# A gated linear recurrence with a dense block behind it: prefix products over the whole sequence in place of pairwise joins of blocks

## The chip, the core and the metric

The kernel runs on one core of a Trainium2 chip. A core has five engines that run side by side, each through its own instructions in order: TensorE (PE in the profile; PEld is its loading of weights), VectorE (DVE), ScalarE (ACT), GpSimd (POOL) and SyncE (SP), which here only starts transfers. The metric is the device time of one execution in microseconds (us), lower is better; the figure is the median of three executions.

## The reference

Inputs `q, k, v, a_re, a_im` are float32 of shape (4, 8, 768, 48): batch B, heads H, steps S, width D. The two weight matrices are float64.

```python
mag = np.sqrt(a_re * a_re + a_im * a_im)
scale = np.minimum(mag, 0.999) / (mag + 1e-06)
a_re_n, a_im_n = (a_re * scale, a_im * scale)
for t in range(S):                                   # complex state S_re + i S_im, D x D per head
    new_re = ar * S_re - ai * S_im                   # ar, ai: a_re_n, a_im_n at step t, per row
    new_im = ar * S_im + ai * S_re
    kv = np.einsum('bhd,bhe->bhde', k[:, :, t], v[:, :, t])
    S_re, S_im = (new_re + kv, new_im)
    y[:, :, t] = np.einsum('bhd,bhde->bhe', q[:, :, t], S_re)
x = y as 3072 tokens of 384
h = x @ w_in                                         # 384 -> 2048
r = np.maximum(h, 0.0)
return (r * r) @ w_out                               # 2048 -> 384
```

In the inputs, `a_re` is uniform between 0.85 and 0.95 and `a_im` is normal with deviation 0.1, so a step shrinks the state by about a tenth.

## The kernel before

Work goes in **units** of one batch, two heads and 384 steps (32 units), and two units make a duo. A unit has head and dim on the 128 partitions (two heads of 48, each padded to 64) and steps along the free axis. It is cut into 3 chunks of 128 steps.

The score of step t with an earlier step s is Re(q_t k_s times the decay from s to t). No decay is ever divided by: blocks of w = 1, 2, 4, .. 64 steps are joined in pairs, seven levels, and each level multiplies `Q` (on DVE), `K` (on POOL) and the blocks' whole decays `T` (on DVE) by complex factors. `times` does one such product in four instructions, lines L297 (two), L300 and L302; `join` calls it:

```python
def join(u, w):
    ...
    times(dve, new, T[:, :, :, 0], ..., (n,), False, "t")
    times(dve, Q, Q, decay(0), (n, w), False, "q")
    ...
        times(pool, K, K, decay(1), (n, w), True, "k")
```

Ahead of each join, `small_scores` (L256 on PE, 32 x 32 pieces, gathered by a masked copy on DVE, L259) or `wide_scores` (L274) take that level's scores. Then `states` (L343 to L367) carries a state between chunks, `outputs` (L380, L385) forms y, and, per 384 tokens, the dense part runs on PE: `turn_x` (L395), `hidden` (L402, 16 blocks of 3 matmuls of 128 x 384) with relu and square on ACT (L405, L406), and `project` (L412, 3 blocks of 16). `normalise` (L205 to L224) prepares `a`, `load` (L180 to L192) starts the transfers on SP, and the weights come in 32 pieces by POOL's queue (L134) and are rounded from float64 by seven DVE instructions a piece (L139 to L151).

The order is written out: units two by two, level by level, with one piece of `work` (weights, then the dense part of the group before) after each level by `some`. A tile framework then fixes each engine's order of instructions, and puts in the waits.

Of the kernel before, what the change touches and what calls it, by code (L numbers as in the profile page):

```python
# [9 lines left out]
F32 = mybir.dt.float32  # L10
I32 = mybir.dt.int32
U32 = mybir.dt.uint32
AF = mybir.ActivationFunctionType
ALU = mybir.AluOpType
PSUM = bass.MemoryType.PSUM


@with_exitstack
def kernel(
# [11 lines left out]
    """y_t = q_t . Re(S_t), S_t = a_t S_{t-1} + k_t v_t, then relu(y w_in)^2 w_out.  # L31

    Within a chunk of 128 steps, the decay from s to t is a product that never leaves
    what it multiplies: blocks of w steps are joined in pairs, w = 1, 2, .. 64.  Before
    a join, Q holds q_t times the decay from the start of t's block up to t, K holds the
    conjugate of k_s times the decay from s to the end of s's block, and T holds each
    block's whole decay; so Re(Q K) is the score of each t of a right block with each s
    of the left block beside it.  Nothing is divided by a decay, and no logarithm is
    taken, so any a will do.  The state S (kept conjugated) passes between chunks.

    The weights may come in float64, as the raw 8 bytes: they are rounded to float32, the
    widest type that the engines compute in, on the chip.

    A unit is one batch, two heads and 384 steps: head, dim on the partitions (a head
    from 0, the other from 64, each with 16 rows of zeros), steps along the free axis.
    """
    nc = tc.nc
    B, H, S, D = q.shape
    C = 128
    NC = 3  # L50
    L = NC * C
    NHALF = S // L
# [3 lines left out]
    DM = H * D  # L56
    FF = moe_w_in.shape[1]
    NM = DM // C
# [27 lines left out]
    # masks[w][s mod 32, t]: 1 where s is in a left block of w steps and t in the right  # L86
    # block beside it (w = 0: s = t), for each of the four blocks of 32 partitions.
# [21 lines left out]
    # keeps a head's rows of the state to that head's columns  # L109
# [6 lines left out]
    # score tiles [s, (head, chunk), t]; the places with s > t stay zero  # L116
# [12 lines left out]
    def load_f64(dst, src):  # L129
        """dst = src, each the two words of a float64, rounded to float32; dst is 0 where  # L130
        that would not be a normal number"""
        shape = list(dst.shape)
        raw = wst.tile(shape + [2], U32, name="raw", tag="raw")
        nc.gpsimd.dma_start(out=raw.rearrange("p a b two -> p a (b two)"), in_=src)  # L134
        lo, hi = raw[:, :, :, 0], raw[:, :, :, 1]
        bits = dst.bitcast(U32)
        more = wst.tile(shape, U32, name="more", tag="more")
        # sign, exponent and the upper 20 bits of the fraction
        dve.tensor_scalar(out=bits, in0=hi, scalar1=0x07FFFFFF, scalar2=3,  # L139
                          op0=ALU.bitwise_and, op1=ALU.logical_shift_left)  # L140
        dve.scalar_tensor_tensor(out=bits, in0=hi, scalar=0xC0000000, in1=bits,
                                 op0=ALU.bitwise_and, op1=ALU.bitwise_or)
        # the lower 32, in units of the exponent
        dve.tensor_scalar(out=more, in0=bits, scalar1=0xFF800000, scalar2=None,
                          op0=ALU.bitwise_and)
        dve.scalar_tensor_tensor(out=more.bitcast(F32), in0=lo, scalar=2.0 ** -52,
                                 in1=more.bitcast(F32), op0=ALU.mult, op1=ALU.mult)
        dve.tensor_tensor(out=dst, in0=dst, in1=more.bitcast(F32), op=ALU.add)
        dve.tensor_scalar(out=more, in0=hi, scalar1=1, scalar2=None,
                          op0=ALU.logical_shift_left)  # L150
        dve.scalar_tensor_tensor(out=dst, in0=more, scalar=float(2 * 897 << 20), in1=dst,  # L151
                                 op0=ALU.is_ge, op1=ALU.mult)
# [42 lines left out]
    def normalise(u):  # L195
        """a *= min(|a|, 0.999) / (|a| + 1e-6)"""
# [11 lines left out]
        # the root's table wants its input in its range; then one Newton step  # L208
# [17 lines left out]
    def turn(u):  # L226
        """steps from the partitions to the free axis"""
# [14 lines left out]
    def small_scores(u, w):  # L242
        """scores of blocks of w within blocks of 32, gathered in u["A"]"""
# [19 lines left out]
    def wide_scores(u, w):  # L263
        """scores of blocks of 32 or 64, straight to their place"""
# [21 lines left out]
    def times(eng, dst, x, t, shape, conj, tag):  # L286
        """dst = x * t or x * conj(t), complex; dst may be x"""
# [17 lines left out]
    def join(u, w):  # L305
        """blocks of w to blocks of 2 w"""
# [26 lines left out]
    def states(u):  # L333
        """S before each chunk of the unit, and the one after it"""
# [137 lines left out]

# [28 lines left out]
```

## Time and profile before

| | |
|---|---|
| times of three runs | 1626.14 us median (1620.57 to 1630.79) |
| profiled execution, first to last instruction | span 1629.0 us |
| DVE busy | 1292.8 us, 79% of the span |
| PE busy | 1124.1 us, 69%, granted clock 0.824 in the mean |
| POOL busy | 848.4 us, 52% |
| ACT busy | 380.6 us, 23% |
| packets moved | 44.02 MB, 27 GB/s in the mean |

The profiled execution is one of its own, not one of the three; its span lies inside their range, 2.9 us above the median. "Busy" counts instructions that run, not those that wait. In a row of the timeline the first two numbers are start and duration; two instructions of one engine overlap a little, so the cost of one in a row of them is the distance from its start to the next one's. In a group's row, "x448 | 293.2, 661 | 0.0" means 448 instructions, 293.2 us busy, 661 ns for one in the mean, and no idle time of the engine ahead of them.

### The profile page before, as it was taken

What the parts mean: (1) busy time and instruction counts of PE and PEld (TensorE: products, weight loads), DVE (VectorE), ACT (ScalarE), POOL (GpSimd) and SP (SyncE); (2) the same over time, 40 slices, a digit from 0 to 9 for tenths busy, and PEclk for the clock granted to TensorE, in tenths of its full rate; (3) what the DMA queues carried; (4) which work ended last, traced back from release to release, by engine and by line L of the source; (5) the groups of instructions that cost most, each with busy time, mean ns of one, the idle gap of its engine ahead of it and who ended that gap; (6) DMA issues with size and microseconds to landing.
All of it is one profiled execution on the core that took longest, in us unless ns stands there. A gap on an engine that the chain in (4) does not pass through costs nothing.

```text
span 1629.0 us, 48569 instructions
## 1 busy us (share of the span) xinstructions
PE 1124.1 (69%) x20840; PEld 765.1 (47%) x20840; DVE 1292.8 (79%) x2922; ACT 380.6 (23%) x858; POOL 848.4 (52%) x1119
## 2 busy tenths in 40 slices
PE   2116215767877769767877779766877779676999
PEld 2115114545454546444454546444554546454565
DVE  6999998998959795988859794988859794979600
ACT  3012010232123311322123311222213321222131
POOL 5653764666627372555637372656537371656400
PEclk9997555878787979778888979778888969778899
DMA  4113212102020100102020200102020200100000
GB/s 93 54 36 82 64 40 64 34 2 39 7 48 2 34 6 21 34 2 39 6 48 3 38 3 23 31 2 39 6 48 3 39 2 26 29 1 3 11 5 14
DMA packets 137301, 44.02 MB, mean 27 GB/s; under 512 B 131456, under 2 KB 134528, under 8 KB 137088
## 3 DMA queue, kind: packets, MB, share of 16 engines
q1 hardware_dynamic: 134016, 28.34, 9.0%
q0 software_dynamic: 3072, 12.58, 2.5%
q8 instruction: 164, 2.69, 0.6%
q14 instruction: 49, 0.40, 0.1%
HBM read 36.18 MB, written 4.72 MB: 25 GB/s over the span
## 4 chain that ended last, share of the span: by engine, by line
DVE 58%; PE 23%; POOL 6%; issue 6%; ACT 4%; DMA 1%; SPq 1%; DVEq 0%; POOLq 0%; ACTq 0%
DVE q L297 13%; PE o L412 11%; DVE t L297 9%; DVE Q L300 6%; DVE Q L302 6%; DVE s L220 4%; PE h L402 3%; DVE A L259 3%; DVE T L300 3%; PE kv L348 2%; DVE T L302 2%; PE y L380 2%; DVE s L215 2%; PE y L385 2%; POOL k L297 2%
## 5 line engine op out<-in xcount | busy, mean ns | idle before, releaser
L297 POOL TENSOR_TENSOR k<-K,T 128x384 f32<-128x384 f32 x384 | 429.6, 1134 | 145.4 <-DVE T L302 57.8
L256 PE MATMUL lv<-Q,K 64*32 64x32 f32 x13824 | 178.8, 222 | 282.8 <-DVE Q L300 134.3
L402 PE MATMUL h<-xT,w 128*128 128x384 f32 x768 | 351.3, 607 | 2.3 <-DVE xT L396 2.3
L256 PEld LDWEIGHTS lv<-Q,K 64*32 64x32 f32 x13824 | 156.2, 121 | 361.5 <-POOL k L297 150.5
L297 DVE TENSOR_TENSOR q<-Q,T 128x384 f32<-128x384 f32 x448 | 293.2, 661 | 0.0
L412 PE MATMUL o<-w,g 128*128 128x384 f32 x768 | 281.9, 524 | 0.0
L402 PEld LDWEIGHTS h<-xT,w 128*128 128x128 f32 x768 | 168.7, 234 | 105.6 <-issue 46.3
L412 PEld LDWEIGHTS o<-w,g 128*128 128x128 f32 x768 | 152.9, 205 | 102.0 <-issue 18.3
L297 DVE TENSOR_TENSOR t<-T 128x384 f32<-128x384 f32 (+6 forms) x448 | 190.9, 459 | 0.0
L274 PE MATMUL lv<-Q,K 64*32 64x32 f32 (+1 forms) x2304 | 72.3, 236 | 162.4 <-DVE Q L300 136.0
L300 POOL TENSOR_TENSOR K<-k,k 128x192 f32<-128x192 f32 x192 | 136.8, 713 | 69.3 <-PE lv L274 64.9
L274 PEld LDWEIGHTS lv<-Q,K 64*32 64x32 f32 (+1 forms) x2304 | 59.6, 144 | 198.7 <-issue 128.3
L239 DVE TENSOR_TENSOR Q<-T,q 128x768 f32<-128x768 f32 x32 | 30.6, 956 | 150.5 <-ACT T L237 150.5
L300 DVE TENSOR_TENSOR Q<-q,q 128x192 f32<-128x192 f32 x224 | 138.5, 618 | 3.3 <-PE lv L274 3.0
L302 POOL TENSOR_TENSOR K<-k,k 128x192 f32<-128x192 f32 x192 | 135.6, 706 | 0.7 <-PE lv L256 0.7
L302 DVE TENSOR_TENSOR Q<-q,q 128x192 f32<-128x192 f32 x224 | 129.7, 579 | 0.0
L405 ACT ACTIVATE g<-h 128x384 f32<-128x384 f32 x128 | 62.3, 486 | 284.0 <-PE h L402 283.9
L185 POOL MEMSET kn<- 128x96 f32 x32 | 5.8, 182 | 196.2 <-PE tp L236 195.0
L284 ACT COPY score<-A 32x192 f32<-32x192 f32 x128 | 44.7, 349 | 151.3 <-DVE A L259 150.2
L207 POOL TENSOR_TENSOR s<-s,s 128x288 f32<-128x288 f32 x32 | 32.7, 1021 | 75.3 <-ACT s L206 75.3
L351 DVE TENSOR_TENSOR add<-kv,own 128x288 f32<-128x288 f32 (+1 forms) x64 | 25.7, 401 | 56.6 <-PE kv L348 56.2
L211 ACT ACTIVATE s<-s 128x288 f32<-128x288 f32 x32 | 14.1, 440 | 235.7 <-DVE s L209 235.7
(86 smaller groups left out, 1637.1 us busy)
## 6 DMA issues: line engine op xcount, KB each, us to landing
raw<-in_moe_w_in_dram POOLq DMA_DIRECT2D x16, 384.0 KB, 3.9
raw<-in_moe_w_out_dram POOLq DMA_DIRECT2D x16, 384.0 KB, 3.3
a<-in_a_re_dram SPq DMA_DIRECT2D x96, 48.0 KB, 2.2
a<-in_a_im_dram SPq DMA_DIRECT2D x96, 48.0 KB, 2.8
qn<-in_q_dram SPq DMA_DIRECT2D x96, 48.0 KB, 2.3
kn<-in_k_dram SPq DMA_DIRECT2D x96, 48.0 KB, 2.2
v<-in_v_dram SPq DMA_DIRECT2D x96, 48.0 KB, 2.0
out_dram<-o SPq DMA_DIRECT2D x24, 192.0 KB, 1.9
```

What stands on the lines that cost most here:

```text
L207: pool.tensor_tensor(out=s1, in0=s1, in1=s2, op=ALU.add)
L220: dve.reciprocal(out=s3, in_=s3)
L256: nc.tensor.matmul(ps[ts(i, SB), h, ts(c, SB)], lhsT=u["K"][rows, j, cols], rhs=rhs, start=(j == 0), stop=(j == parts[-1]))
L259: dve.copy_predicated(out=u["A"].rearrange("p (h c) t -> p h (c t)", h=2), mask=masks[w].rearrange("p (h c) t -> p h c t", h=2), data=ps[: ...
L274: nc.tensor.matmul(ps[lo:lo + w, h, ts(c, w)], lhsT=u["K"][rows, j, left], rhs=u["Q"][rows, j, right], start=(j == 0), stop=(j == 1))
L284: act.copy(out=u["score"][ts(i, SB), :, ts(i, SB)], in_=u["A"][ts(i, SB)])
L297: eng.tensor_tensor(out=f, in0=x, in1=part, op=ALU.mult)
L300: eng.tensor_tensor(out=dst[:, 0], in0=ra[:, 0], in1=rb[:, 1], op=ALU.add if conj else ALU.subtract)
L302: eng.tensor_tensor(out=dst[:, 1], in0=ra[:, 1], in1=rb[:, 0], op=ALU.subtract if conj else ALU.add)
L402: nc.tensor.matmul(ps, lhsT=w1[:, m, ts(f, C)], rhs=g["xT"][:, m], start=(m == 0), stop=(m == NM - 1))
L405: act.activation(out=t, in_=ps, func=AF.Relu)
L412: nc.tensor.matmul(ps, lhsT=g["h"][f][:, ts(c, C)], rhs=w2[:, f], start=(f == 0), stop=(f == NF - 1))
```

## The change

The old kernel becomes `general_path`, unchanged but for its name and comments. A new `fast_path` runs first, always, and writes the whole output; it ends in a number `flag`, and `general_path` runs only where that is not 0.

```diff
+    fast_path(tc, *args, flag)
+    bad = nc.values_load(flag[0:1, 0:1], min_val=0, max_val=1)
+    with tc.If(bad > 0):
+        general_path(tc, *args)
```

The fast path takes the product P_t of all decays from step 0 to t, and sets Q~ = q P and K~ = k P / |P|^2; then every score is one plain matmul. P starts at 2^59, 1/|P|^2 at 2^-118 (`x`). The checks (`grow`, `total`, `sums`, `odd`, put together in `verdict`) ask that sums and products stay in range, `x` at most 2^124 at the end among them.

Its unit is one batch, all 8 heads and 384 steps: 8 units. Steps are on the partitions, 3 to each. A unit's **chain** (`chain_work`) is: `load`; `normalise` (logarithm and exponential on ACT instead of root and reciprocal); `inner`, the products within each partition's 3 steps; `inverse`, one over the squared size; `totals`, a turn of each partition's product to 96 rows by 128; `scan`, the prefix products along these 128 by groups of 8, on DVE; `back`, a turn back; `apply` and `rotate`, which make Q~ and K~.

```diff
+    def product(u, dst, x, y):
...
+            dve.tensor_tensor(out=t, in0=x, in1=y[:, j].unsqueeze(1).to_broadcast(shape),
+                              op=ALU.mult)
...
+        dve.tensor_tensor(out=dst[:, 0], in0=f[0][:, 0], in1=f[1][:, 1], op=ALU.subtract)
+        dve.tensor_tensor(out=dst[:, 1], in0=f[0][:, 1], in1=f[1][:, 0], op=ALU.add)
+    def scan(u):
...
+        for w in range(1, 8):
+            product(u, v8[:, :, :, :, w], v8[:, :, :, :, w - 1], v8[:, :, :, :, w])
...
+        for w in range(1, 4):
+            product(u, i4[:, :, :, :, w], i4[:, :, :, :, w - 1], i4[:, :, :, :, w])
+        for g in range(1, 4):
...
+            product(u, i4[:, :, :, g], i4[:, :, :, g], for_all)
+        for i in range(NP):
...
+            product(u, v8[:, :, i, 1:16], v8[:, :, i, 1:16], y)
```

A unit's **pair work** (`pair_work`, four pairs of heads) is `turn` (12 transposes a pair), `score`, `keep` (the state for the other half, first halves alone) and `mix` (y, turned already, which SP's transfers put in place as `xT`). The **dense work** is as before, 48 + 48 matmuls of 128 x 384 a unit.

```diff
+    def score(u, i):
...
+        for h in range(2):
...
+            nc.tensor.matmul(sa[:, 0:3].rearrange("p n t -> p (n t)"), lhsT=kt[:, 0:C],
+                             rhs=qt, start=True, stop=True)
+            nc.tensor.matmul(sa[:, 3], lhsT=kt[:, 2 * C:3 * C], rhs=qt[:, 2 * C:3 * C],
+                             start=True, stop=True)
+            nc.tensor.matmul(sb[:, h].rearrange("p n t -> p (n t)"), lhsT=kt[:, C:2 * C],
+                             rhs=qt[:, C:3 * C], start=True, stop=True)
+            dve.tensor_tensor(out=A[:, h, 0:4:3], in0=sa[:, 0:4:3], in1=mask2, op=ALU.mult)
+            act.copy(out=A[:, h, 1:3], in_=sa[:, 1:3])
...
+    def mix(u, i):
...
+        if late:
+            for h in range(2):
+                nc.tensor.matmul(ypair[64 * h:64 * h + D], lhsT=state[u["b"]][:, 2 * i + h],
+                                 rhs=T[:, h], start=True, stop=False)
+        for j, lo, hi in ((0, 0, 3), (1, 4, 6), (2, 3, 4)):
+            for h in range(2):
+                nc.tensor.matmul(ypair[64 * h:64 * h + D, j * C:L],
+                                 lhsT=u["v"][:, j, 2 * i + h],
+                                 rhs=A[:, h, lo:hi].rearrange("p n t -> p (n t)"),
+                                 start=(j == 0 and not late), stop=(j == 2))
```

Three stages run at once: the dense work of unit n, the pair work of n + 1 and the chain of n + 2, merged evenly. The weights are rounded by five DVE instructions a piece (`convert`) beside the first pair work and the second chain, and their exponents checked by loading them again (`inspect`, two DVE instructions a piece). The inputs `a`, `qk` and the chain's own tiles have one buffer each, so the next unit's load waits for `rotate`.

```diff
+    for f in chain_work(units[0]):
+        f()
+    merge(pair_work(units[0]),
+          [lambda i=i: convert(i) for i in range(NPIECE)])
+    merge(chain_work(units[1]), [lambda i=i: convert(i) for i in range(NPIECE, 2 * NPIECE)])
+    for n, u in enumerate(units):
+        lists = [dense_work(u)]
+        if n + 1 < NU:
+            lists.append(pair_work(units[n + 1]))
+        if n + 2 < NU:
+            lists.append(chain_work(units[n + 2]))
+        elif n + 1 < NU:
+            lists.append([lambda i=i: inspect(i) for i in range(2 * NPIECE)])
+        merge(*lists)
```

What this makes of the engines' order shows at three places. On PE, before the change, in the middle of a group (lv: score pieces; h, o: the dense part):

```order
L256 MATMUL lv<-Q,K 32x32 x48
L402 MATMUL h<-xT,w_153 128x384
L256 MATMUL lv<-Q,K 32x32 x48
L412 MATMUL o<-w_154,g 128x384 x5
L274 MATMUL lv<-Q,K 32x32 x24
L412 MATMUL o<-w_154,g 128x384 x7
```

On PE after it, in the middle of a unit (tq: a pair's turn; sa, sb: its scores; ypair: its y; tot and bk: the chain's turns):

```order
L903 MATMUL h<-xT,w_109 128x384 x3
L709 MATMUL tot<-ident,last 96x128 x8
L903 MATMUL h<-xT,w_109 128x384
L709 MATMUL tot<-ident,last 96x128 x4
L816 MATMUL tq<-ident,QK 96x128 x4
L903 MATMUL h<-xT,w_109 128x384 x5
...
L915 MATMUL o<-w_110,g 128x384 x8
L869 MATMUL ypair<-A,v 48x384 x2
...
L832 MATMUL sa<-QKT 128x128
L834 MATMUL sb<-QKT 128x256
L779 MATMUL bk<-ident,e 128x96 x8
```

The small score pieces, which waited for a join each, are gone; the chain's turns stand among the dense matmuls, 40 of the 48 h ahead of the first.

On DVE, before the change, at a join during the weights' rounding (t, q: products; A: scores; L139 and L141: a weight piece):

```order
L297 TENSOR_TENSOR q_782<-Q,T_615 128x384
L139 TENSOR_SCALAR w_153<-raw 128x3x128
L300 TENSOR_TENSOR Q<-q_780,q_782 128x48x4
L302 TENSOR_TENSOR Q<-q_780,q_782 128x48x4
L141 SCALAR_TENSOR_TENSOR w_153<-raw,w_153 128x3x128
```

On DVE after it, in the first unit's scan (L743, L746, L747: a product; L578 to L586: a weight piece):

```order
L743 TENSOR_TENSOR fa<-e,inc 96x240 x2
L582 TENSOR_SCALAR more<-w_109 128x384
L746 TENSOR_TENSOR e<-fa 96x120
L747 TENSOR_TENSOR e<-fa 96x120
L584 SCALAR_TENSOR_TENSOR more<-raw,more 128x384
L743 TENSOR_TENSOR fa<-e,inc 96x240 x2
L586 TENSOR_TENSOR w_109<-w_109,more 128x3x128
```

The roundings moved into the chains: up to the end of the first unit's `rotate` stand 71 of the 160 instructions of rounding, the other 89 in the second unit's chain, and 59 of the 64 of `inspect` in the third's.

On ACT after it, where a chain begins amid the end of a unit (L632 to L646: `normalise`; yt: y of a pair; ot: the output; h: the next unit's relu). Before the change ACT had one table load at L205 and one at L211 in all:

```order
L839 COPY A<-sb 128x2x128
L632 ACTIVATE fa,sums<-a 128x2304
L636 ACT_TABLE_LOAD
L636 ACTIVATE fa<-fb 128x1152
L637 ACT_TABLE_LOAD
L637 ACTIVATE fa<-fa 128x1152
L638 ACTIVATE fb,sums<-fa 128x1152
L640 ACTIVATE fb<-fa 128x1152
L874 COPY yt<-ypair 112x384
L645 ACTIVATE fa<-fb 128x1152
L919 COPY ot<-o 128x384
L646 ACTIVATE fa<-fb 128x1152
L906 ACTIVATE g<-h 128x384
```

The next unit's first relu stands behind the whole of `normalise`'s part on ACT; four table loads come in each chain. On SP, the load of `a_im` stands behind that of `a_re`, an output and the three `xT` transfers of a pair.

More of the change, by code (lines that the diff above doesn't have):

```diff
@@ L15, with general_path @@
 PSUM = bass.MemoryType.PSUM
+AX = mybir.AxisListType.X
+AXY = mybir.AxisListType.XY
 @with_exitstack
-def kernel(
+def general_path(
     ctx: ExitStack,
@@ new lines, with kernel @@
+@with_exitstack
+def kernel(
+    ctx: ExitStack,
+    tc: tile.TileContext,
+    q: bass.AP,
+    k: bass.AP,
+    v: bass.AP,
+    a_re: bass.AP,
+    a_im: bass.AP,
+    moe_w_in: bass.AP,
+    moe_w_out: bass.AP,
+    out: bass.AP,
+):
+    nc = tc.nc
+    fp = ctx.enter_context(tc.tile_pool(name="flag", bufs=1))
+    flag = fp.tile([1, 1], I32, name="flag")
+    args = (q, k, v, a_re, a_im, moe_w_in, moe_w_out, out)
+    fast_path(tc, *args, flag)
+    bad = nc.values_load(flag[0:1, 0:1], min_val=0, max_val=1)
+    with tc.If(bad > 0):
+        general_path(tc, *args)
```

381 lines of the change are left out of this document (added).

## The prediction

> **What bounds the kernel now.** First the page: how much of the span each engine is busy, and the chain of work that ended last.
>
> ```profile
> span 1629.0 us, 48569 instructions
> PE 1124.1 (69%) x20840; PEld 765.1 (47%) x20840; DVE 1292.8 (79%) x2922; ACT 380.6 (23%) x858; POOL 848.4 (52%) x1119
> DVE 58%; PE 23%; POOL 6%; issue 6%; ACT 4%; DMA 1%; SPq 1%; DVEq 0%; POOLq 0%; ACTq 0%
> ```
>
> DVE holds the path; next, the groups by line and what PE waits for.
>
> ```profile
> L297 POOL TENSOR_TENSOR k<-K,T 128x384 f32<-128x384 f32 x384 | 429.6, 1134 | 145.4 <-DVE T L302 57.8 <-DVE K L325 54.2 <-DVE T L300 29.4
> L297 DVE TENSOR_TENSOR q<-Q,T 128x384 f32<-128x384 f32 x448 | 293.2, 661 | 0.0
> PE lv L274 <- DVE Q L300: 136.0, 39, 15.5
> PE lv L256 <- DVE Q L300: 134.3, 52, 13.1
> ```
>
> Read: the joins of Q fill DVE, and PE's score pieces wait for them. The two waits alone are 270 us. The third view is the timeline with the stages' granted clock: at the end the dense part runs alone, in the middle it is mixed with the rest.
>
> ```profile
> 1563.16 31.23 PE L402 MATMUL h<-xT,w 128*128 128x384 f32 x96 [1.25 <-DVE xT L396]
> 1594.22 31.12 PE L412 MATMUL o<-w,g 128*128 128x384 f32 x96
> 1570.00:1600.00 30.00, 30.00 (x94) 17.67 (x93) 0.00 (x0) 13.49 (x27) 0.00 (x0) 1.00 0.00 1
> 1241.00:1500.00 259.00, 193.00 (x3765) 130.21 (x3763) 214.27 (x468) 68.04 (x154) 141.24 (x185) 0.83 0.08 16
> 170.00:180.00 10.00, 0.00 (x0) 0.00 (x0) 10.00 (x19) 0.00 (x0) 7.54 (x10) 0.50 0.20 58
> ```
>
> Read: a unit's dense work (48 + 48 matmuls, each of them two records) takes 62.2 us (31.23 to the start of the second row, then 31.12) at clock 1.00; mixed, the clock is 0.83, and where PE idles it is 0.50. Eight units are 498 us, so whatever is done to the joins leaves that much.
>
> **The change: PE.** From the first of those rows, a record of 384 columns costs 31.23 / 96 = 0.325 us, 0.85 ns a column; a matmul is two. For transposes and short matmuls:
>
> ```profile
> 736.29 0.49 PE L236 MATMUL tp<-ident,kn 128*128 128x128 f32 x3
> 736.62 0.49 PE L236 MATMUL tp<-ident,qn 128*128 128x128 f32 x3
> 730.96 0.54 PE L380 MATMUL y<-v,score 128*128 128x48 f32 x4
> 731.34 0.65 PE L385 MATMUL y<-S,Q 128*128 128x96 f32 x4
> ```
>
> A transpose costs 0.33 / 3 = 0.11 us (start to start), a 48-column matmul 0.38 / 2 = 0.19. A unit then has on PE: dense 62.2; `turn`, 48 transposes, 5.3; `totals` and `back`, 24, 2.6; `score`, 8 heads of 384 + 128 + 256 columns, 1.30 each, 10.4; `mix` the same 10.4 in a first half and 15.6 in a second (384 columns more a head), 13.0 in the mean; `keep` 24 x 0.19 in first halves, 2.3. Sum **95.8 us**, eight units 766. What goes from PE costs no time by itself, since PE waited there.
>
> **DVE.** With POOL at rest and with POOL at work:
>
> ```profile
> 154.40 0.96 DVE L239 TENSOR_TENSOR Q<-T,q 128x768 f32<-128x768 f32 x1 [2.20 <-ACT T L237]
> 155.27 0.55 DVE L148 TENSOR_TENSOR w<-w,more 128x384 f32<-128x384 f32 x1
> 160.45 0.35 DVE L300 TENSOR_TENSOR T<-t,t 128x192 f32<-128x192 f32 x1
> 160.72 0.35 DVE L302 TENSOR_TENSOR T<-t,t 128x192 f32<-128x192 f32 x1
> 1506.01 0.17 DVE L300 TENSOR_TENSOR T<-t,t 128x24 f32<-128x24 f32 x1
> 1506.10 0.17 DVE L302 TENSOR_TENSOR T<-t,t 128x24 f32<-128x24 f32 x1
> 1513.83 1.66 DVE L297 TENSOR_TENSOR q<-Q,T 128x384 f32<-128x384 f32 x2
> ```
>
> 768 elements cost 0.87 us start to start, 192 cost 0.27, 24 cost 0.09: 0.07 us and 1.04 ns an element. Beside POOL the same 384 that should be 0.47 take 0.83. POOL does no arithmetic in the fast path, so I use the first. A unit: `normalise` four of 1152 (1.27 each) and one of 2304, 7.6; `inner` four of 768 and four of 384, 5.4; `inverse` 5.1; `totals` and `scan` 12.5 (14 of 128, 14 of 64, 8 each of 240 and 120, 26 below 33, four scans of 128); `apply` seven of 1152, 8.9; `rotate` eight of 576, 5.4; masks of the scores, twelve of 256 at 0.37, 4.4. Sum **49 us** a unit, half of PE's. A rounding instruction is 0.44 (they lie between 0.27 and 0.47, as the 384 above), so 160 are 70 us; `inspect`'s 64 I take at 0.4. No row has its reduction, nor the scan instruction: the low end is nothing above these, the high end the reciprocal's price (below), 6.7 ns an element, 68 us more for 32 reductions and 2.6 a unit for the scans. I take the plain one, since both read a row once as those do, and keep the high end for the range.
>
> **ACT.**
>
> ```profile
> L220 DVE RECIPROCAL s<-s 128x288 f32<-128x288 f32 x32 | 62.1, 1941 | 0.0
> L406 ACT ACTIVATE g<-g 128x384 f32<-128x384 f32 x128 | 66.9, 523 | 3.3
> L211 ACT ACTIVATE s<-s 128x288 f32<-128x288 f32 x32 | 14.1, 440 | 235.7 <-DVE s L209 235.7
> L211 ACT ACT_TABLE_LOAD x1 | 1.3, 1283 | 0.0
> ```
>
> 523 less 440 ns for 96 elements is 0.86 ns an element, so 1152 cost 1.18 us and 2304 cost 2.2. With four table loads (5.1) a unit comes to 9.3 + 8.1 in the chain, 16.2 for 16 relus and squares, some 22 for copies: about 61 us. No bound either; logarithm and exponential I price as the root of L211.
>
> **The chain of one unit.** What matters is that it has one set of buffers, so chains run one after the other: load 7 (below), `normalise` 20 (ACT 2.2, DVE 1.3, two tables and three functions 6.1, square 1.2, DVE 2.7, two copies 2.3, DVE 3.8, hops), `inner` 5.4, `inverse` 12.6, `totals` 2.2, `scan` 11.3, `back` 2, `apply` and `rotate` 14.3. Sum **75 us** with nothing in the way.
>
> ```profile
> a<-in_a_re_dram SPq DMA_DIRECT2D x96, 48.0 KB, 2.2
> 10.00:20.00 10.00, 0.76 (x48) 0.62 (x48) 5.84 (x15) 2.64 (x7) 7.86 (x17) 1.00 0.74 171
> raw<-in_moe_w_in_dram POOLq DMA_DIRECT2D x16, 384.0 KB, 3.9
> ```
>
> The load: 171 GB/s at a share of 0.74 is 231 GB/s, so the 1.18 MB of `a` take 5.1 and 2.2 to land; 7. At the start, beside the first weights, 11.
>
> **The sum by stages.** (1) The first chain: 11, DVE 45 (49 without masks), 71 roundings 31, and 12 in which DVE waits for ACT with nothing to fill in: rotate ends at 99. The weights' pieces land in 3.9 with two buffers, faster than 14 in 88 us are used. (2) The second chain: 7, DVE 49, 89 roundings 39, gaps 9: 203. The first pair work and dense work, 96 of PE, lie beside it. (3) The third: 7, 49, 59 of `inspect` 24, gaps 15: 298. PE's order puts the second unit's dense matmuls behind this chain's turns, so PE has only the second pair work (some 34) to do in these 95 and idles some 60. From **300** on PE is full.
> (4) Five more chains, each beside one unit's 95.8 of PE. The chain's 75 would fit, but its parts stand in fixed places of PE's and ACT's queues. Following one round: `tot` stands behind 40 of 48 h and two pairs, some 39 us of PE (26 for the h, 13 for the pairs' turns, scores and a y); `bk` 18 later; then `back`, `apply` and `rotate` 17; the load 7; and `normalise`'s ACT part, 16, stands ahead of the next unit's first relu. Queued behind it are the relus, and with two PSUM buffers for h PE can run 4 us ahead. 39 + 18 + 17 + 7 + 16 = 97 against 95.8 + 4. The two just meet, so I add 5 for the wait at tables and hops: **101** a unit, 805 at the end of the last rotate.
> (5) Left on PE: 19 of the unit before, 96, the last dense work 62; then 3.6 for copy and output, as now,
>
> ```profile
> 1625.43 0.48 ACT L415 COPY o<-o 128x384 f32<-128x384 f32 x1 [9.89 <-PE o L412]
> ```
>
> and the flag and branch, for which there is no row: between 0 and 7 (a transfer's 2.2 and a few hops), I take 3. In all 805 + 184 = **989**. The span of 1629.0 stands 2.9 above the median, so I leave it: **990 us**, 0.61 of now.
>
> [...] The row at 170 us shows 0.50 with PE idle, that at 1570 shows 1.00 with PE full. [...]
>
> **Rivals.**
> *A. PE's column halves run together.* `mix` puts two heads into different column halves, one behind the other.
>
> ```profile
> 1501.21 0.88 PE L256 MATMUL lv<-Q,K 64*32 64x32 f32 x80 [0.37 <-DVE Q L302]
> 986.44 1.00 PE L274 MATMUL lv<-Q,K 64*64 64x64 f32 x20
> ```
>
> For: 80 records of 32 columns in 0.88 us are 11 ns each, against 27 by columns. Against: 20 of 64 in 1.00 are 50 against 54, no gain. If so, `mix` halves, PE is 89.3 a unit, a round 92, and the sum 300 + 5 x 92 + 15 (rest of a unit) + 89 + 62 + 7 (copy, flag) = 933. Chance 0.15. [...]
> *B. The clock stays as in the mixed stage now*, 0.83: for it speaks that 0.83 is what 259 us with PE 75% busy had, and that PE will still wait for ACT here and there; against it the last stage, full and at 1.00. 95.8 / 0.83 = 115, a round 118: 300 + 5 x 118 + 22 + 115 + 62 + 7 = 1096. Chance 0.12.
> *C. The chain does not overlap.* If the load of `a_im`, behind three `xT` transfers on SP, comes only when PE is done with a unit, each round pays load and `normalise`, 23, on top of 95.8: 119, and about 1077. For: SP's order. Against: `xT` is not the last of a unit. Chance 0.11.
> *D. The branch is taken.* If one check fails the old kernel runs behind the new: 989 + 1629 = 2618, slower than now. It decides at 1/|P|^2 = 2^124 in any of 1536 rows, or at a weight's exponent. Shrinking by a tenth in 768 steps makes 2^-118 to about 2^104; over the reference's own inputs the largest I work out is 2^112, and no weight is out of range. Chance 0.02. Nothing in the profile speaks on it.
>
> **How the numbers follow.** Forecast 0.60, A 0.15, B 0.12, C 0.11, D 0.02. Three runs spread over 0.6%, so below 1% either way is no change. All but D are faster: 0.97; within 1% 0.01; slower 0.02. The range: A less a smoother start, where roundings fill every gap, 910, to B with 15 more for the reductions (68 on DVE in the third stage, mostly beside waits), 1110.
>
> **What would show it.** Right: PE's clock near 1.00 from 300 on; dense groups 8 x 62; `tot`, `bk` without long waits; rotate every 101 us. Rotate's ends at 99, 203, 298 test the first stages. Wrong: a clock of 0.8 in the middle (B); PE waiting for ACT's relu by more than 5 a unit, behind DMA of `a` (C); L869 pairs that start together (A); any line of the old joins in the trace (D).

## The result and the profile after

The changed kernel takes 953.69 us (median of four runs, 949.63 to 957.55) where the kernel before takes 1627.34 (four runs, the profiled one counted too, 1620.57 to 1630.79): a ratio of 0.5865, 95% interval 0.584 to 0.5891. The forecast was 990 in a range of 910 to 1110, so the direction and the range held and the time is 36 us shorter than forecast. The executions of one kernel differ by up to 1%, and a profile shows one of them, here the one of 956.58; so differences of a few us between two profiles are read beside the medians. First the page of the changed kernel: span, busy time by engine, the granted clock in 40 slices, the chain of work that ended last.

```profile
span 954.8 us, 8914 instructions
PE 784.0 (82%) x3138; PEld 470.4 (49%) x3138; DVE 534.2 (56%) x1223; ACT 458.4 (48%) x753; POOL 43.3 (5%) x76
PEclk9999998997567999999999999999999999999999
PE 42%; DVE 25%; ACT 17%; DMA 8%; issue 6%; SPq 0%; POOL 0%; ACTq 0%; POOLq 0%; DVEq 0%
```

DVE fell from 1292.8 us to 534.2 and from 58% of the path to 25%; PE now has 42% of the path and is busy for 82% of the span. The clock row (a digit for each slice of 23.9 us) is low at one place, slices 10 to 13 (215 to 310 us), with one 8 in slice 7 besides. The stages are cut at the ends of `rotate` (L804), the last step of a chain. Of its rows, those that end the third, the fourth and the last chain (start, duration):

```profile
297.91 2.75 DVE L804 TENSOR_TENSOR QK<-qk,a 128x576 f32<-128x576 f32 x4
384.59 2.76 DVE L804 TENSOR_TENSOR QK<-qk,a 128x576 f32<-128x576 f32 x4
779.26 2.76 DVE L804 TENSOR_TENSOR QK<-qk,a 128x576 f32<-128x576 f32 x4 [3.42 <-PE kv L853]
```

All eight ends, read the same way: 93.9, 202.2, 300.7, 387.3, 482.1, 585.4, 683.1 and 782.0. Between the third and the last lie five rounds of 96.3 us in the mean, and 172.8 us follow. The windows of these stages (length, then busy time of PE, PEld, DVE, ACT and POOL, the granted clock, DMA share, GB/s):

```profile
0.00:94.00 94.00, 9.60 (x39) 6.46 (x39) 82.00 (x188) 28.61 (x33) 13.71 (x28) 1.00 0.41 111
94.00:202.00 108.00, 97.33 (x385) 58.97 (x385) 88.36 (x213) 57.01 (x96) 11.02 (x19) 0.95 0.37 112
202.00:301.00 99.00, 57.46 (x207) 32.37 (x206) 76.60 (x187) 40.28 (x57) 18.56 (x29) 0.66 0.49 146
301.00:387.00 86.00, 81.55 (x345) 49.03 (x344) 55.32 (x125) 53.95 (x91) 0.00 (x0) 0.96 0.19 52
387.00:782.00 395.00, 373.22 (x1557) 225.65 (x1557) 225.41 (x498) 224.72 (x375) 0.00 (x0) 0.98 0.16 44
782.00:955.00 173.00, 164.80 (x614) 97.97 (x610) 6.55 (x17) 53.78 (x105) 0.00 (x0) 0.99 0.05 15
```

In the third stage PE idles 41 of 99 us at a clock of 0.66. From the fourth on it is 94% busy or more. What PE waits for in the four full rounds (387 to 782), in us in total, times, longest:

```profile
PE h L903 <- ACT g L906: 7.3, 8, 1.7
PE bk L779 <- DVE e L746: 6.3, 8, 1.2
PE h L903 <- DMA xT<-yt: 4.9, 3, 2.6
PE tot L709 <- ACT e L711: 1.2, 1, 1.2
PE bk L779 <- ACT xn L780: 1.1, 2, 0.6
```

That is 21 us in four rounds, no wait longer than 2.6. None of the old joins' lines is in the trace.

### The profile page after: what moved, and what is told of

Read it like the earlier page. It is cut to its first block, busy times and chain, and to the rows that moved or that the text cites. A ratio compares the mean times of both kernels' runs of the same rounds, so it can differ in the third digit from the quotient of the medians.

```text
span 954.8 us, 8914 instructions
## 1 busy us (share of the span) xinstructions
PE 784.0 (82%) x3138; PEld 470.4 (49%) x3138; DVE 534.2 (56%) x1223; ACT 458.4 (48%) x753; POOL 43.3 (5%) x76
## 4 chain that ended last, share of the span: by engine, by line
PE 42%; DVE 25%; ACT 17%; DMA 8%; issue 6%; SPq 0%; POOL 0%; ACTq 0%; POOLq 0%; DVEq 0%
PE o L915 15%; PE h L903 14%; DVE fa L743 6%; DMA a<-in_a_im_dram 3%; PE ypair L869 3%; PE sa L830 3%; DMA raw<-in_moe_w_in_dram 3%; PE tq L816 2%; DMA raw<-in_moe_w_out_dram 2%; DVE e L746 2%; ACT fa L672 2%; DVE fa L661 1%; PE sb L834 1%; ACT QKT L819 1%; ACT g L906 1%
## 5 line engine op out<-in xcount | busy, mean ns | idle before, releaser
L903 PE MATMUL h<-xT,w 128*128 128x384 f32 x768 | 273.7, 502 | 24.6 <-ACT g L906 12.8
L819 ACT COPY QKT<-tq 96x512 f32<-96x512 f32 x96 | 81.1, 854 | 86.0 <-PE tq L816 85.7
L836 DVE TENSOR_TENSOR A<-sa,mask 128x256 f32<-128x256 f32 x64 | 26.9, 422 | 130.8 <-PE sa L832 130.5
L816 PE MATMUL tq<-ident,QK 128*96 128x128 f32 x384 | 63.7, 293 | 13.3 <-DVE QK L804 10.4
L816 PEld LDWEIGHTS tq<-ident,QK 128*96 128x96 f32 x384 | 47.1, 135 | 44.4 <-issue 25.4
L907 ACT ACTIVATE g<-g 128x384 f32<-128x384 f32 x128 | 66.5, 523 | 2.7
L830 PE MATMUL sa<-QKT 96*128 96x384 f32 x128 | 58.6, 542 | 3.0 <-ACT QKT L819 2.9
L869 PE MATMUL ypair<-A,v 128*48 128x256 f32 (+2 forms) x384 | 56.6, 388 | 4.3 <-ACT A L837 4.3
L804 DVE TENSOR_TENSOR QK<-qk,a 128x576 f32<-128x576 f32 x64 | 43.9, 752 | 16.8 <-PE kv L853 8.5
L743 DVE TENSOR_TENSOR fa<-e 96x128 f32<-96x128 f32 (+1 forms) x120 | 40.0, 368 | 14.4 <-ACT e L711 13.3
L869 PEld LDWEIGHTS ypair<-A,v 128*48 128x48 f32 x384 | 25.6, 123 | 38.3 <-issue 22.0
```

Source lines behind the costliest of these rows:

```text
L743: dve.tensor_tensor(out=t, in0=x, in1=y[:, j].unsqueeze(1).to_broadcast(shape), op=ALU.mult)
L804: dve.tensor_tensor(out=t[:, j, :, :, r], in0=u["qk"][:, j, ts(z, HH)], in1=u["a"][:, r, ts(z, HH)], op=ALU.mult)
L816: nc.tensor.transpose(ps[:, 2 * j + h], src[:, j, (2 * i + h) % HH, c].rearrange("p r d -> p (r d)"), ident)
L819: act.copy(out=u["T"][i].rearrange("r z (p c) -> r c z p", c=W)[:, c], in_=ps)
L830: nc.tensor.matmul(sa[:, 0:3].rearrange("p n t -> p (n t)"), lhsT=kt[:, 0:C], rhs=qt, start=True, stop=True)
L836: dve.tensor_tensor(out=A[:, h, 0:4:3], in0=sa[:, 0:4:3], in1=mask2, op=ALU.mult)
```

## The experiments

The theory on trial, P: after the third `rotate` TensorE's own work is the pace, and the chain sets only the first three stages. Its rival, C: the chain of VectorE and ScalarE sets every round. Ratios below are to the kernel before, on the same chip.

### e1: more work on PE

```diff
         ps = dp.tile([C, L], F32, name="h", tag="d")
+        if f % 2 == 0:
+            nc.tensor.matmul(ps, lhsT=w1[:, 0, ts(f, C)], rhs=u["xT"][:, 0],
+                             start=True, stop=True)
```

> Adds to every unit's dense work 8 matmuls of 128 x 384 whose result is overwritten, 5.2 us of PE a unit (16 records of 0.325). Theory P (from 300 us on PE's work sets the pace, and the chain fits beside it): the seven units from there on each become 5.2 longer, 954 + 36 = 990; the rotate ends from the fourth chain on stand 101 us apart instead of 96. Rival C (the chain's loop of load to rotate with one set of buffers sets the pace, and PE only fills it): the five rounds keep 96, only the last two dense works grow, 954 + 10 = 964.

979.51 us (979.36 to 983.21; ratio 0.6044). The first three ends stay (94.0, 200.2, 298.8); the rounds grow from 96.3 to 99.3, the end stage from 172.8 to 182.3. The window of the four full rounds:

```profile
386.00:795.50 409.50, 391.59 (x1634) 238.51 (x1632) 225.07 (x497) 228.50 (x377) 0.00 (x0) 0.98 0.16 43
```

PE has 97.9 us a round now in place of 93.3, and idles 4.5 in place of 5.4. The 26 us are most of the 36 that P asks for where PE is the pace throughout, and more than C's 10. The fourth round takes nothing of it (87.0 against 86.7), the four full ones 3.8 each.

### e2: a longer chain

```diff
-        dve.tensor_tensor(out=flat(a[:, 0]), in0=flat(fa[:, 0]), in1=flat(fb[:, 1]),
-                          op=ALU.subtract)
+        for _ in range(5):
+            dve.tensor_tensor(out=flat(a[:, 0]), in0=flat(fa[:, 0]), in1=flat(fb[:, 1]),
+                              op=ALU.subtract)
```

> Does one subtraction of 1152 elements in apply five times instead of once: 4 x 1.27 = 5.1 us more of DVE in every chain, the result unchanged. Theory P: the first three chains, which PE waits for, cost 15 more, the five later ones are hidden beside PE's work, 954 + 16 = 970. Rival C: all eight chains cost 5.1 more, 954 + 41 = 995.

967.76 us (965.7 to 967.85; ratio 0.596). The third end moves from 300.7 to 311.5; the five rounds after it are 96.3 in the mean, as before (the four full ones 97.8 against 98.7). So the chain is the pace up to the third end and has 5 us to spare in a round: P.

### e3: one column half after the other

`mix` writes the two heads of a pair into two column halves of PE (rows 0 to 47 and 64 to 111 of `ypair`), by turns. Here all of one head's matmuls come first.

```diff
-        for j, lo, hi in ((0, 0, 3), (1, 4, 6), (2, 3, 4)):
-            for h in range(2):
+        for h in range(2):
+            for j, lo, hi in ((0, 0, 3), (1, 4, 6), (2, 3, 4)):
```

> In mix all matmuls of one head stand ahead of those of the other, so neighbours share a column half instead of alternating. If the halves run together now (12 records of a first half's pair took 1.43 us where columns alone would need 2.6, and 16 of a second half's 2.1 where 3.9), a pair gets 1.2 to 1.8 longer, a unit about 6: theory P then gives six units times 6, 954 + 36 = 990; rival C about 962, since only PE's slack is used up. If the halves do not run together, and the short mix has another cause, mix keeps its length: 954.

960.88 us (957.09 to 961.84; ratio 0.5924, 0.5906 to 0.5941, against the changed kernel's 0.584 to 0.5891). The timeline of PE, a group of twelve records of `mix`, of the changed kernel, and its first 0.3 us alone:

```profile
384.83 1.50 PE L869 MATMUL ypair<-A,v 128*48 128x384 f32 x12
386.26 0.91 PE L830 MATMUL sa<-QKT 96*128 96x384 f32 x2
...
384.83 0.53 PE L869 MATMUL ypair<-A,v 128*48 128x384 f32 x2
```

and the same of e3:

```profile
380.99 2.18 PE L868 MATMUL ypair<-A,v 128*48 128x384 f32 x12
383.11 0.91 PE L830 MATMUL sa<-QKT 96*128 96x384 f32 x2
...
380.99 0.52 PE L868 MATMUL ypair<-A,v 128*48 128x384 f32 x1
```

Then the instructions at `ypair` alone (`mix` on PE, PEld, DVE and ACT) in the four full rounds, first of the changed kernel, then of e3; and last all of e3's instructions in them:

```profile
387.00:782.00 395.00, 27.91 (x214) 12.60 (x216) 0.00 (x0) 7.10 (x15) 0.98 0.16 44
383.46:776.01 392.55, 43.36 (x213) 21.11 (x214) 0.00 (x0) 7.34 (x16) 1.00 0.16 44
383.46:776.01 392.55, 380.33 (x1557) 230.73 (x1556) 225.05 (x497) 225.67 (x376) 0.00 (x0) 1.00 0.16 44
```

Start to start, 1.43 us by turns and 2.12 one after the other; and by turns the first two records, one of each head, start together (x2 in the short row), where in e3 one starts alone. So the halves do run together, with a gain of 1.48 here. But the time rose by 7 us only. In the full rounds `mix` takes 10.8 us a round in place of 7.0, and yet the rounds are no longer (98.1 against 98.7): PE is idle 3.1 us a round in place of 5.4, and its clock is 1.00 in place of 0.98, so that it is busy only 1.8 longer. What grows is the end stage, by PE's busy time (171.5 us against 164.8): 179.4 against 172.8. (The profiled execution of e3 is the shortest of its four, so its span, 955.4, shows 0.6 of the 7 us.) The expectation of 990 was wrong; e12 takes this up.

### e4: the inspection after the last chain

The second reading of the weights (`inspect`) gets buffers that the chains use, so that it can only run when they are done.

```diff
-        dst, _, hi = load_raw(i)
+        late = nat.tile([C, 2, H, W, D], F32, name="late", tag=("a", "qk")[i % 2])
+        raw = late.rearrange("p r h c d -> p (r h c d)").bitcast(U32)[
+            :, 0:shape[1] * shape[2] * 2].rearrange("p (a b two) -> p a b two",
+                                                    b=shape[2], two=2)
+        nc.gpsimd.dma_start(out=raw.rearrange("p a b two -> p a (b two)"), in_=src)
```

> The weights' second loading for inspect goes into the buffers of a and qk, so that it can only come after the last chain's rotate, beside the last two dense works. If DVE's queue sets the third chain's length, 59 instructions of about 0.4 leave it, its rotate ends at 278 instead of 301, and the time falls by 20 to 24 to about 932, the end costing nothing as DVE idles there. Rival: the third stage is set by PE's slow clock (0.66 there) and the second pair work, or by transfers; then the time stays at 954.

952.79 us (947.55 to 957.58; ratio 0.5882), no difference that can be told from the changed kernel. The profiled execution is the shortest of its four, with a span 9 us below that of the changed kernel; it shows a gain and a loss. The third end is 16 us earlier, at 284.7, and the last one 22 earlier, at 759.6 in place of 782.0, but 186 us follow in place of 172.8. The third chain without the inspection, and a piece of the end stage with it:

```profile
202.00:285.00 83.00, 53.21 (x211) 30.20 (x210) 56.59 (x126) 40.84 (x58) 0.00 (x0) 0.74 0.13 37
...
780.00:800.00 20.00, 14.74 (x58) 9.26 (x56) 9.25 (x22) 7.27 (x15) 6.42 (x9) 0.96 0.67 181
800.00:820.00 20.00, 19.63 (x72) 11.63 (x73) 8.71 (x20) 9.53 (x18) 4.96 (x9) 0.87 0.62 186
820.00:840.00 20.00, 17.61 (x68) 9.82 (x67) 7.28 (x19) 7.61 (x15) 2.69 (x5) 0.91 0.37 114
```

Where the changed kernel's PE is busy without a gap and at 1.00, it now idles some 8 us and drops to 0.87, at a DMA share of 0.6 to 0.7. The wait that shows is for ACT (`h` for `g`, 8.0 us in two pieces); what held ACT there was not separated further.

### e5: a second buffer for the chain's input

```diff
-        u["a"] = nat.tile([C, 2, H, W, D], F32, name="a", tag="a")
+        u["a"] = nat.tile([C, 2, H, W, D], F32, name="a", tag="a", bufs=2)
```

Paid for with single buffers for `yt`, `ot`, `S` and `more`.

> A second buffer for the tile `a`, into which a unit's qk is loaded, paid for with single buffers for yt, ot, S and more. The load (5.6 us, with the wait for its buffer up to 7) then stands ahead of the chain and not in it. Theory P (TensorE sets the rounds, the chain has slack): the rounds stay at 95 to 97 us, only the second and third chain end some 5 us earlier each, 943 to 954 us. Theory C (the chain of VectorE and ScalarE sets the rounds): 7 us less in each of five rounds and 10 in the start, 905 to 920 us. A third outcome, over 958 us, would say that the single buffers of yt and ot cost more than the load.

934.64 us (932.42 to 936.74; ratio 0.5755, 0.5729 to 0.5782): 19 us less than the changed kernel, more than P foresaw and less than C. By the profiles it is 24: the ends are 95.0, 198.9, 283.4, 366.1 and on to 758.0, so 17 us are won by the third end, 4 in the fourth round, 3 in the other four together, and none in the end stage (172.7). Where the third chain gains, on ACT and DVE, in the changed kernel (`rotate` ends at 202.2):

```profile
210.45 2.12 ACT L632 ACTIVATE fa<-a 128x2304 f32<-128x2304 f32 x1 [2.60 <-DMA a<-in_a_im_dram]
216.71 0.36 DVE L594 TENSOR_SCALAR more<-raw 128x384 uint32<-128x384 uint32 x1 [4.71 <-DMA raw<-in_moe_w_in_dram]
216.99 1.35 DVE L634 TENSOR_TENSOR fb<-fa 128x1152 f32<-128x1152 f32 x1
```

and in e5 (`rotate` ends at 198.9):

```profile
198.79 1.35 DVE L634 TENSOR_TENSOR fb<-fa 128x1152 f32<-128x1152 f32 x1
```

L634 starts 14.8 us after the `rotate` before, and in e5 at once. Of the 14.8, 8.2 are the load (until L632 starts) and 2.1 the square; most of the rest is a wait of 4.7 of DVE for a piece of `inspect` (L594), which stands ahead of L634 in its queue and whose transfer had not landed. In e5 the load and the square move under the unit before, and L634 stands ahead of these pieces. The four full rounds stay at 98:

```profile
366.00:758.00 392.00, 371.57 (x1564) 226.40 (x1562) 223.43 (x497) 220.97 (x373) 0.00 (x0) 0.98 0.15 41
```

A third chain that is 14 us shorter (84.5 against 98.5), and no load to wait for in any later one, leave them alone, which is P again. This is the fastest version that was run.

### e6: e4 and e5 together

> The late inspection of e4 and the second buffer of e5 in one kernel. If the two gains are of different waits they add: e4's rotate 22 us earlier, of which 9 reached the end, and e5's 5 to 10, so 935 to 945 us. If TensorE's own 790 us with its start of 94 are the floor, nothing under 930 is left; if the inspection in the last stage costs what it saves in the third, 947 to 954 as e4.

945.13 us (941.45 to 947.63; ratio 0.5821, 0.5796 to 0.5845): 10 us more than e5 alone. The third end is 8 us earlier than e5's (275.5), the last 4 (754.2 in place of 758.0), where e4 alone gained 16 and 22; and the end stage is 186 again. The expectation that both gains add was wrong: they share a part (the wait of 4.7 for an inspection piece, shown at e5, is one that either change takes away), and the loss of e4 stays.

### e7: the same work, unit by unit

```diff
+    for n, u in enumerate(units):
+        for f in chain_work(u):
+            f()
...
+        for f in pair_work(u):
+            f()
+        for f in dense_work(u):
+            f()
```

> The same work without the three-stage order: unit by unit its chain, its pairs, its dense part, and the inspection at the end. If the order of the lists is what hides the chain, each round is chain 75 plus TensorE's 90 us, less what the engines' own queues still let run ahead: all in a row 8 x (75 + 95) + some 60 = 1420 us; with the part of the next chain that needs no TensorE running beside the dense part (some 45 of its 75), 1060 to 1120 us. If the queues alone would overlap it all, 954 to 970.

1186.42 us (1184.14 to 1197.18; ratio 0.7317). Rounds are some 139 us; the queues still let a part of the next chain run ahead, but less than the 1060 to 1120 foresaw. Two rounds:

```profile
533.30:671.20 137.90, 103.83 (x379) 59.96 (x377) 56.49 (x126) 55.62 (x92) 0.00 (x0) 0.85 0.11 30
671.20:811.40 140.20, 105.67 (x410) 64.54 (x409) 55.80 (x123) 56.93 (x96) 0.00 (x0) 0.84 0.12 34
```

and the longest of PE's waits in them:

```profile
PE bk L779 <- DVE e L746: 33.3, 8, 14.8
PE tq L816 <- DVE QK L804: 20.1, 4, 9.9
```

PE idles 34 us a round with waits of up to 14.8, and at a clock of 0.84 the same work takes it 105 us, where the changed kernel's full rounds, at 0.98, take 93. Those have no wait above 2.6; but they hold four stretches of some 3.4 us at half the clock. One of them:

```profile
463.60:467.00 3.40, 3.40 (x9) 2.19 (x9) 3.40 (x3) 0.95 (x3) 0.00 (x0) 0.50 0.00 0
```

Three of the four begin at the `bk` turns (here after waits of 0.6, 1.2 and 0.6 us between short turns), one after the wait of 2.6. With the same 72 transposes a round e3 has a clock of 1.00 in its full rounds; whether the turns or the short waits bring these stretches was not tested. Each costs 1.7 us of PE by estimate (3.4 us at half the clock), some 7 in the four rounds.

### e8: no branch in the program

```diff
-    bad = nc.values_load(flag[0:1, 0:1], min_val=0, max_val=1)
-    with tc.If(bad > 0):
-        general_path(tc, *args)
```

> The flag is computed, but the program holds no general path and no branch, so it would be of use only for inputs within the range. If the branch costs only its read of the flag and the jump, the end after the last copy falls from 7.5 to some 3.1 us: 949 to 951 us. If the general path's code behind the branch costs more than that (loading of a longer program, buffers that it takes from the fast path), more than 10 us less.

951.6 us (949.17 to 952.06; ratio 0.5851, 0.5826 to 0.5876): by the times no different from the changed kernel. In the profile 3.0 us lie between the last output's start and the end of the span, in the changed kernel, shown here, 7.5:

```profile
946.77 0.48 ACT L919 COPY ot<-o 128x384 f32<-128x384 f32 x1 [9.88 <-PE o L915]
946.84 0.15 DVE L979 TENSOR_SCALAR flag<-cnt 1x1 int32<-1x1 f32 x1 [74.21 <-PE cnt L978]
947.27 0.33 SPq L921 DMA_DIRECT2D out_dram<-ot  x1
```

So by the profile the flag and the branch cost about 4.5 us, and the long code behind the branch nothing that shows.

### e9: the inspection spread over the rounds, with e5

```diff
+        pool.tensor_copy(out=raw[:, 0, 0:1, 0].bitcast(F32), in_=u["g"][-1][:, 0:1])
         nc.gpsimd.dma_start(out=raw.rearrange("p a b two -> p a (b two)"), in_=src)
...
+        if 1 <= n < NU - 2:
+            per = range((n - 1) * 7, min(n * 7, 2 * NPIECE))
+            lists.append([lambda i=i, u=u: inspect(i, u) for i in per])
```

> The second buffer of e5, and the inspection spread over the second to sixth round, six or seven pieces a round: GpSimd touches each piece's buffer with a column of the newest tile g before the load, so that no piece can be read ahead of its round. If a round is set by TensorE alone and VectorE has room in it (56 of 97 us busy), the third chain shortens as in e6 (last rotate 4 to 8 us earlier than e5's 758) and the end stage stays at 173: 922 to 930 us. If the 0.9 us of VectorE and the 384 KB of a piece delay the chain or the loads of xT inside a round, the gain is given back: 934 to 945.

938.73 us (938.28 to 938.97; ratio 0.5785, 0.5762 to 0.5808), not faster than e5. The third end is 6 us earlier than e5's (277.6), but the fourth round is 90.2 us long in place of 82.7, and the last end is 6 later (764.0). The fourth round and the four later ones:

```profile
277.60:367.85 90.25, 84.42 (x345) 51.70 (x345) 59.35 (x135) 53.55 (x91) 9.00 (x14) 0.92 0.29 80
367.85:763.99 396.14, 374.37 (x1557) 227.22 (x1557) 240.47 (x549) 223.90 (x373) 23.25 (x50) 0.97 0.23 65
```

In the fourth round PE's clock is 0.92 and it is busy 84.4 us, in e5 1.00 and 76.6; so the earlier end wins nothing there. In the later rounds PE is busy 93.6 a round against e5's 92.9, at a clock of 0.974 against 0.983, which is the same work. They are 1 us longer each; what lowers the clock in either place was not settled. Three places for the inspection were tried, and none is free.

### e10: the old kernel without GpSimd's joins

```diff
-            times(pool, K, K, decay(1), (n, w), True, "k")
+            pass
```

> The kernel before without the multiplications by which GpSimd joins K (the K that it uses is then unjoined, so this part is left out of the computation). Theory N: VectorE's own count of instructions set the old time, 1293 of 1626 us busy: unchanged within 3%, 1580 to 1640 us. Theory S: GpSimd's joins slowed VectorE beside them: VectorE's busy time falls by 200 us or more and the time with it, to 1350 to 1450 us.

1307.04 us (1305.66 and 1308.41; ratio 0.8054, 0.8012 to 0.8097). DVE's groups of the joins, before:

```profile
L297 DVE TENSOR_TENSOR t<-T 128x384 f32<-128x384 f32 (+6 forms) x448 | 190.9, 459 | 0.0
L300 DVE TENSOR_TENSOR Q<-q,q 128x192 f32<-128x192 f32 x224 | 138.5, 618 | 3.3 <-PE lv L274 3.0 <-DVE neg L354 0.3
```

and here, the page's line of the engines first:

```profile
PE 1010.1 (77%) x20840; PEld 701.2 (54%) x20840; DVE 974.4 (75%) x2922; ACT 378.9 (29%) x858; POOL 176.6 (14%) x351
```

```profile
L297 DVE TENSOR_TENSOR t<-T 128x384 f32<-128x384 f32 (+6 forms) x448 | 105.1, 268 | 0.0
L300 DVE TENSOR_TENSOR Q<-q,q 128x192 f32<-128x192 f32 x224 | 80.2, 358 | 15.7 <-PE lv L256 9.3 <-PE lv L274 6.0 <-DVE neg L354 0.3
```

The same 2922 instructions of DVE take 974 us in place of 1293, and DVE's idle time stays (330 us, before 336), so the time falls with its busy time: theory S, and further than its 1350 to 1450. One and the same instruction (L300) takes 618 ns in the mean with GpSimd's joins and 358 without them. So some 316 of the old kernel's 1623 us (on this run's chip) go with GpSimd's joins, by slower instructions of VectorE; what it is in the joins that slows them was not shown. The fast path leaves GpSimd out of the arithmetic (43 us busy in all); how much of the change's gain is due to that, and how much to the joins that are gone, no run separates.

### e11: the branch taken

```diff
-        dve.tensor_scalar(out=flag, in0=ps, scalar1=C - 0.5, scalar2=None, op0=ALU.is_lt)
+        dve.tensor_scalar(out=flag, in0=ps, scalar1=C + 0.5, scalar2=None, op0=ALU.is_lt)
```

> The flag's limit is set so that the flag is always raised: the fast path runs, and the old kernel behind it. If the old kernel starts cold after the flag, 950 + 4 + 1620 = some 2575 us; if it shares the weights' loads or overlaps with the end, 50 or more below; if the branch's code comes in more slowly than the first kernel's, above 2600.

2571.61 us, one run: 948.3 more than the kernel before on the same chip (1623.27). The fast path is paid in full and the old kernel after it; its first instruction starts 1.2 us after the flag is written:

```profile
943.70 0.15 DVE L979 TENSOR_SCALAR flag<-cnt 1x1 int32<-1x1 f32 x1 [74.22 <-PE cnt L978]
...
945.04 0.20 POOL masks.py:197 MEMSET ident<- 128x128 f32 x1 [661.69 <-ACT ot L919]
```

### e12: e3 on top of e5

> e3's order of `mix` (one column half after the other) on top of e5's second buffer, so that the chain is further ahead and TensorE has less to wait for. In e3 the groups of twelve took 2.12 us in place of 1.43, some 4 us a unit, but the time rose by 7 us only. If waits for the chain had swallowed the rest there, they are fewer here, and it costs 4 us or more for each of some seven units: 960 to 970 us, rounds of 100 and more. If TensorE's waits shrink by as much again (for other reasons than the chain), 938 to 945, with rounds of 97 to 98 and less idle in them than e5's 5 us each. If the order costs nothing, 930 to 937.

954.12 us (951.52 to 957.01; ratio 0.5879, 0.5855 to 0.5904): 19.5 us more than e5, where e3 cost 7 on the changed kernel. In the profile, of 22 us of span, 10 come up to the third end (293.2), 6 in the five rounds and 6 in the end stage (179.2). It lies between the two cases foreseen: the first three stages and the end stage grow, while the four full rounds are 98.8 (e5 98.0) where the dearer case had 100 and more, because PE's idle time shrinks again (3.5 us a round, e5 5.1):

```profile
378.38:773.58 395.20, 381.04 (x1566) 232.37 (x1562) 223.29 (x496) 220.90 (x373) 0.00 (x0) 1.00 0.15 41
```

96% busy, at 1.00. In the second and third stage DVE waits for the scores `sa` (L836) 17.5 us in place of e5's 11.8, in e3 12.2 in place of 11.5; so a part of the 10 is the chain waiting for PE, and why it shows in e12 alone stays open. What a microsecond on PE costs depends on how much of it falls on waits and on low clock that are there anyway. Of some 42 us added in e1 26 reached the time, of some 29 in e3 only 7, and of some 32 in e12 19.

## Why the prediction was right, and where it was off

**The bound moved as said.** DVE's path was replaced by PE's, the old lines are gone, and P held in e1, e2 and e5. What happened is the forecast's course with rival A's `mix` in it, 36 us faster than the forecast's number: 990 to 953.69 (A's 933 lies nearer, 21 below). By the profile it is 989 to 954.8, which splits as +1 up to the third end (300.7 against 300), -24 in the five rounds (481.3 against 505) and -11 behind them (172.8 against 184).

**Stages 1 to 3: 99, 203, 298; measured 93.9, 202.2, 300.7.** The sums hold within some 5 us, though in part by terms that cancel. The third stage without its inspection was 7 + 49 + 15 = 71 in the sum and is 82 in e4, where DVE is busy 56.6 us (in the full rounds 56.4 a unit) and not 49. The inspection then adds 16, not 24, since a part of it fills waits. Left open by the rows of before were the reduction and the scan; for the reduction the plain price was about right, and the scan's 460 ns are above the plain 0.2 us of 128 elements and below the reciprocal's 0.86:

```profile
L596 DVE TENSOR_REDUCE odd<-more 128x1 f32<-128x384 uint32 x32 | 17.5, 547 | 0.4
L714 DVE TENSOR_TENSOR_SCAN x<-tot,x,ones 96x128 f32<-96x128 f32 x32 | 12.9, 460 | 2.4 <-PE tot L709 2.4
```

**Behind the third end the sum gives PE 5 x 95.8 + 19 + 96 + 62 = 656 us of work; 620 were measured.** So the shorter time is PE's work, by terms of which two were too large and one too small.

*`mix`, 13.0 a unit, is the step that failed.* It was priced by columns, one head behind the other. The column halves run together, and it takes 7.0 a unit; behind the third end 47 us in place of 78, which is 31 less. This is rival A's term (6.5), to which the prediction gave a chance of 0.15.

*The rest of the unit before, 19, was counted twice.* Step 4 takes five whole units up to the last rotate, and step 5 adds 19 of the last of them again. The records of `o` show it (48 matmuls of two records, 96 a unit). In the fourth round and in the end stage PE's busy time and count for them, with clock and DMA, are:

```profile
301.00:387.00 86.00, 24.24 (x64) 0.96 0.19 52
782.00:955.00 173.00, 74.10 (x224) 0.99 0.05 15
```

At the fourth rotate 32 of a unit's 96 are still to come, and as many at the last one (224 = 2 x 96 + 32). So the fourth round has 81.6 us of PE where each later one has 93.3, and is 86.7 long in place of 101. The 96 after it also hold chain turns and a `keep`, which the last unit no longer has. Together that is 22 too much.

*The other terms are 17 too low in sum (31 + 22 - 17 = 36).* The unit without `mix` is 86 where 83 was foreseen; by estimate about half of this is the clock (at 0.98, 86 us hold 84 at 1.00), the rest was not separated.

**Step 3, "idles some 60".** PE idled 41 us. It had not done more (8 of the 192 records of the next dense work); it was busy 57.5 us, at a clock of 0.66, and a last part of the first unit's dense work, 26 records of `o`, still fell into it.

**Step 4: the right number of idle time for the wrong reason.** 5 us a round were added because the path through the queues, 97, was to just meet PE's. The idle time is 5.4, but the path is not that long: with 5.1 us more of chain (e2) and with the load out of it (e5) the full rounds are 97.8 and 98.0 against 98.7. That the two numbers agree is luck. The waits are short hops at `h`, `bk` and `xT`, as the list of waits shows.

**Flag and branch** were 3 and are 4.5 by the profile, inside the 0 to 7.

**The rivals.** A's mechanism and its price of `mix` hold, and its sign, records of L869 that start together, is in the trace. Its 933 did not follow: it shares the other terms of PE, too low in both, and has 2.7 us of idle time a round where 5.4 were measured. B is excluded, the rounds run at 0.98; with waits of up to 14.8 us, as in e7, the clock was 0.84. C is excluded by the round itself, 96.3 where C had 119; how it looks when a chain does not overlap is seen in e7, 1186. D costs what was said, 2572 against 2618, and did not happen on these inputs.

**Not foreseen at all:** that the next gain lay in the first three chains, not in PE's rounds. One more buffer, of a tile that the prediction named as the reason why chains run one after the other, is worth 19 us.

## What to carry to other kernels

Before counting instructions of a full VectorE, look at what GpSimd does beside it: the same instruction took 618 ns with GpSimd's joins beside it and 358 with the joins left out, and the old kernel's time fell by a fifth without them (316 of 1623 us). When the bound moves to an engine whose work is pipelined over units, look at the start, where the pipeline is not yet full and the chain alone is the pace: a second buffer for the chain's input won 19 us there, most of it before the third end, and the rounds stayed as they were. When two matmuls write different column halves of PE, issue them by turns: the same twelve records took 1.43 us so and 2.12 one half after the other. And move work that is off the path only after measuring the place where it goes; the inspection was put in three places, and each time what was won in one stage was lost in another.

## What the hardware showed that was not expected

- Twelve fp32 records into alternating column halves take 1.43 us, the same twelve half by half 2.12, where 2.6 were expected by columns at the price of full-width matmuls. So that price holds for neither order.
- A square with a sum on ACT brings an instruction of its own behind it, here 0.18 us, which the prediction left out:

```profile
212.48 0.18 ACT L632 ACTIVATION_READ_ACCUMULATOR fa<-a 128x1 f32 x1
```

- A program with a second kernel of some 48,000 instructions behind a branch that is not taken is no slower by the times than one without it (951.6 and 953.69, with overlapping ranges).
